# A fused attention and two-MLP kernel: the scores of four units read keys in place, the last two w_mid tiles are converted last, and the hand-written order of block 0 is replaced

## The chip, the cores and the metric

The kernel runs on one core of a Trainium2 chip. The metric is device time in microseconds (us), median of several executions. A core has a matrix engine (PE, with its weight loads shown as PEld), a vector engine (DVE), a scalar engine (ACT), a general engine (POOL) and SP, which here only issues DMAs. Each engine works through its own list of instructions in order and waits where an operand is not there yet.

## The reference, cut to what matters

```python
def reference(**kwargs):
    attn_out = _attn_ref(...)     # q, k, v: 4 x 8 heads x 768 x 64; 8 memory keys and values per head
    x = attn_out.transpose(0, 2, 1, 3).reshape(B * S, H * D)          # 3072 x 512
    x = maximum(maximum(x @ w1, x @ w2), x @ w3) @ w_mid              # 512 -> 768 -> 512
    h = x @ w_in                                                      # 512 -> 2048
    g = where(h >= 1, h, where(h <= -1, 0, (h + 1) ** 2 / 4))
    return g @ w_out                                                  # 2048 -> 512

def _attn_ref(q, k, v, mem_k, mem_v):
    for c in range(nc):           # 24 chunks of 32 queries; keys from 16 before to 8 after the chunk, and 8 memory keys
        scores = scale * q_c @ concat(mem_k, k_ctx).T
        a = exp(scores - max(scores)); a = a / (sum(a) + 1e-9)
        out[:, :, c_start:c_end] = a @ concat(mem_v, v_ctx)
```

## The kernel before, in words

The 3072 tokens are six blocks of 512; a block is four attention units of 128 tokens, so there are 24 units. Every matmul of the MLPs is done as three passes on operands split into a rounded high part and a low rest (`mm3`, lines 499 to 501), so every weight tile must first be converted on the chip.

**Weights of the first MLP.** w1, w2, w3 and w_mid (in the profile their fetches are `in_moe_w_dram` and `in_moe_w_out_dram`) are cut into 24 tiles of 512 KB, fetched by `f0` to `f23`; two neighbouring tiles make a pair q, and pair 0 to pair 11 go through the steps `wa` (ACT, L134), `wr` (ACT, L138), `wc` (three DVE instructions, L142, L143, L145), `wd` (DVE, L150), `wh` (ACT, L199) and `ws` (DVE, L204). Only two pairs can be staged at once: the fetch of pair q+2 waits for `wd` of pair q. The list `round1` sets which tile is which: before, a0, a1, a2, b for each of six columns f, where a0, a1, a2 are w1, w2, w3 and b is w_mid.

**An attention unit u** goes through loads `lk`, `lq` (keys, queries, 256 KB each) and `lv` (values, eight DMAs of up to 56 KB); key transposes `tk` (PE, L273), copy `ck` (ACT, L276), the edges shared with the neighbouring unit `ek`; query transposes `tq` (L304) and copy `cq` (L366); `kw` (ACT, L298, and once per batch L287), which lays the memory keys and the four overlapping windows of keys side by side; scores `s` (64 small instructions, L378); `mx` (DVE, L392, L393); `ex` (ACT, L397); `n` (DVE, L401 to L404); transposes `a` (L410) and copy `ca` (L414); `o` (64 small instructions, L426); `cx` (ACT, L436) and `dx` (DVE, L440), which write the high and low part of the MLP's input.

**Block 0.** `PLAN` is one list of step names, written out by hand; a program emits the steps in that order, and each engine gets its own part of it in that order. It holds units 0 to 7, the first step of unit 8, the conversion of all 12 pairs, the first layer of block 0 (`l0` to `l17`, 12 matmuls each, three `l` per column f; `lt` is the running maximum, `lh` the split) and its second layer (`m0` to `m5`, 12 matmuls each; column f needs w_mid's tile f). `d3` and `d7` are four matmuls without a use. `l0` needs pair 0 and all four units of block 0 (`dx3`), so it is the first matmul of the MLPs.

**After the plan** `order` lists slots of 12 matmuls for blocks 1 to 5: `slot_l1(j, f, m)` and `slot_l2(j, f)`. Each slot also takes one step of the attention of later units (`att_step`; two in slots 2 and 3), up to two `evictions` of a finished second layer, and one part of the conversion of a pair of the second MLP (`round_step`, `BY_PART`).

Of the kernel before, what the change touches and what calls it, by code (L numbers as in the profile page):

```python
# [37 lines left out]


PLAN = """  # L40
d3 lk1 d3 lmem0 d3 d3 lk0 d3 lm0 lq0 lv1 tk1 mem0 ck1 tk0 ck0 ek1 tq0 lk2 kw0 d3 mv2 cq0 lq1 lk3 s0
mv0 mx0 lq2 tk2 mv1 ck2 ek2 lk4 tq1 ex0 lv0 cq1 n0 tk3 kw1 ck3 s1 ek3 a0 kw2 mx1 tq2 lq3 tk4 cq2 f0
ck4 f1 s2 ex1 lk5 f2 d3 ek4 mx2 f3 kw3 lq4 lv2 ca0 n1 tq3 ex2 o0 cq3 n2 a1 cx0 s3 ca1 dx0 wa0 mx3 o1
wr0 tk5 wc0 a2 cx1 d7 d7 ca2 d7 ex3 d7 dx1 ck5 d7 d7 ek5 wd0 kw4 n3 wa1 tq4 f4 cq4 lv3 wc1 wr1 s4
wh0 o2 kw5 wd1 a3 d7 cx2 d7 ws0 f5 wh1 d7 lq5 f6 dx2 ca3 f7 mx4 lk7 o3 lv4 ws1 ex4 d7 cx3 d7 n4 wa2
tq5 wr2 dx3 a4 wc2 cq5 ca4 s5 l0 wa3 wd2 wr3 mx5 f9 l1 f8 wh2 lv5 wc3 ex5 lt0 o4 n5 l2 cx4 lt1 ws2
lq7 a5 lq6 wd3 ca5 l3 lm1 wa4 dx4 lk6 f11 lt2 wr4 f10 wc4 l4 lh2 lt3 wh3 wd4 tq7 o5 cq7 ws3 f13 wh4
f12 tk6 mv6 l5 cx5 ws4 lk8 ck6 lv6 dx5 wa5 lt4 tq6 lt5 wr5 m0 wc5 cq6 lh5 wa6 l6 wd5 wr6 wc6 lq8 f14
wh5 f15 tk7 l7 lt6 lk9 ck7 ws5 ek7 kw6 wd6 l8 lt7 f16 wh6 f17 ws6 s6 lt8 wa7 m1 mx6 wr7 wc7 lh8 ex6
tq8 l9 cq8 wa8 wd7 m2 wr8 wc8 f18 f19 lt9 wh7 l10 wd8 ws7 f21 wh8 f20 n6 tk8 l11 ck8 ek8 lt10 kw7  # L50
ws8 wa9 tk9 lt11 l12 wr9 wc9 ck9 wa10 a6 lh11 wd9 l13 ek9 wr10 f22 f23 wc10 ca6 lt12 m3 wh9 wd10 o6
ws9 wh10 s7 lt13 cx6 lv7 ws10 wa11 l14 mx7 wr11 kw8 dx6 l15 lq10 lt14 ex7 lk10 wc11 lk11 lh14 lm2
lq9 l16 lt15 wd11 m4 n7 wh11 ws11 a7 lt16 l17 ca7 o7 lt17 lh17 s8 cx7 dx7 m5 mx8 ex8 f24 f25 f26 f27
""".split()

ON_DVE = """
# [8 lines left out]
def attention_then_two_mlps(ctx, tc, q, k, v, mem_k, mem_v, w1, w2, w3, w_mid, w_in, w_out, out):  # L65
    nc = tc.nc
# [35 lines left out]
    weights = {}  # L102
    wsrc = {"a0": w1, "a1": w2, "a2": w3, "b": w_mid, "c": w_in, "d": w_out}
    wsrc = {n: w.bitcast(U32) for n, w in wsrc.items()}
    round1 = [(m, f) for f in range(K1) for m in ("a0", "a1", "a2", "b")]
    round2 = [(m, f + h) for m in "dc" for f in range(HF) for h in (0, HF)]
    conv = round1 + round2
    Q1, Q2, Q3 = len(round1) // 2, (len(round1) + K2) // 2, len(conv) // 2
# [106 lines left out]
    few = at.tile([P, 2 * HP, 1], F32, name="few")  # L215
    held = {"kw": None}
    qn, kn, pt, rs, aT, pm, pp, px = {}, {}, {}, {}, {}, {}, {}, {}
    xh, xl = {}, {}
# [151 lines left out]
    def st_s(u):  # L370

        ub = u % UPB
        t = [banks[i] for i in spots["s"]]
        for h in range(HP):
            for c in range(NC):
                for e in range(2):
                    r, i = slice(e * 64, e * 64 + 64), h % 2 * 2 + h // 2
                    nc.tensor.matmul(  # L378
                        t[e][c * CH:(c + 1) * CH, i * NK:(i + 1) * NK], qTb[u % 2][r, h, c], kw[r, h, c, 0:NK],
                        start=True, stop=True)  # L380
        b = spots["s"][0]
        pp["s", u] = sg = psums[:, b:b + 2, 0:HP * NK].rearrange("p e (h j) -> p e h j", h=HP)
        if ub == 0:
            nc.vector.memset(sg[0:CH, :, :, NM:NM + LEFT], FLOOR)
        if ub == UPB - 1:
            nc.vector.memset(sg[P - CH:P, :, :, NK - RIGHT:NK], FLOOR)

    def st_m(u):
        sg = pp.pop(("s", u))
        pt[u] = at.tile([P, 2 * HP, NK], F32, tag="p", name=f"p{u}", bufs=2)  # L390
        m, p = [x.rearrange("p (e h) j -> p e h j", e=2) for x in (few, pt[u])]
        nc.vector.tensor_reduce(out=m, in_=sg, axis=AX.X, op=ALU.max)  # L392
        nc.vector.tensor_tensor(out=p, in0=sg, in1=m.to_broadcast([P, 2, HP, NK]), op=ALU.subtract)  # L393

    def st_e(u):
        p = pt[u]
        nc.scalar.activation(out=p, in_=p, func=AF.Exp, scale=scale)  # L397

    def st_n(u):
        p = pt[u]  # L400
        nc.vector.tensor_reduce(out=few, in_=p, axis=AX.X, op=ALU.add)  # L401
        nc.vector.tensor_scalar(out=few, in0=few, scalar1=1e-9, scalar2=None, op0=ALU.add)
        nc.vector.reciprocal(out=few, in_=few)
        nc.vector.tensor_tensor(out=p, in0=p, in1=few.to_broadcast([P, 2 * HP, NK]), op=ALU.mult)  # L404
# [33 lines left out]
    def cp_xl(u):  # L438
# [54 lines left out]
    def att_step():  # L493
        for s in todo.pop() if todo else ():
            run(*s)
# [480 lines left out]
    with tc.manual_schedule(engines={ENG.PE, ENG.DVE, ENG.Activation, ENG.Pool, ENG.SP}):  # L976
# [67 lines left out]
        def w_tile(name):  # L1044
            return wpool.tile([P, 2, TB], F32, tag="w", name=name)

        last_block = done = 0
        for s, (f, *a) in enumerate(order):
            j = a[0]
            if f is not slot_l2 and j == NB - 1 and last_block == 0:  # L1050
# [28 lines left out]
            if last_block:  # L1079
                t = s - last_block  # L1080
                round_step(["out"])
                if t == 1:
                    for g in (2, 3):
                        hq["h22", g] = w_tile(f"h22_{g}")
                for name in LAST_BLOCK.get(t, "").split():
                    if name == "c":
                        split_c()
                    elif name == "raw":
                        load_c(loaded[0])
                        loaded[0] += 1  # L1090
                    elif name == "r":
                        load_d(t - 4)
                    elif name == "d":
                        i = len(resident)
                        split_d(i)
                        if i + 2 < len(RESIDENT):
                            load_d(i + 2)
                    elif name == "E":
                        hq["h21", 0] = w_tile("h21_0")
                    else:  # L1100
                        prep(0, name)
            else:
# [87 lines left out]
```

## Time and profile before

| | us |
|---|---|
| median of 3 runs (lowest, highest) | 962.3 (962.0, 962.8) |
| the profiled execution's own time | 960.31 |
| its span, first to last instruction | 958.5 |
| PE busy in the span | 938.7 |

The profiled execution has 1.8 us around its span. Times in the rows are counted from the span's start. A row of the timeline gives start, duration, engine, line, operation, what is written and read, the shapes and the number of merged instructions; in brackets the idle time of that engine before it and what ended it. An instruction may begin before the one ahead of it has fully ended, so the step from start to start is what a series costs.

### The profile page before, as it was taken

To read this page: it belongs to the slowest core of one execution; us is meant where nothing else is said; L and a number is where in the kernel's file an instruction comes from. 1 tells how busy PE (TensorE), PEld (TensorE's weight loads), DVE (VectorE), ACT (ScalarE), POOL (GpSimd) and SP (SyncE) were. 2 spreads that over 40 slices of the span, in tenths; PEclk is the share of its full clock that TensorE was granted. 3 is DMA by queue.
4 is the path that set the end of the run, shared out by engine and by line. 5 is a ranking of instruction groups with operands and counts; after the bars stand their busy time and mean duration, and the time that the engine had idled before them with its cause. 6 is when DMAs were issued, how large, how long until landed. Compare 5 with 4: busy or idle time off the path is not lost.

```text
span 958.5 us, 18892 instructions
## 1 busy us (share of the span) xinstructions
PE 938.7 (98%) x7090; PEld 772.4 (81%) x7090; DVE 704.6 (74%) x1001; ACT 541.9 (57%) x972; POOL 339.6 (35%) x330
## 2 busy tenths in 40 slices
PE   6799999999999999999999999999999999999998
PEld 5588887888888888888888888888888888888886
DVE  3999857687877777753337778997777988777855
ACT  5767554333343324223447777776777776777763
POOL 0000003221321111111746555555565555655642
PEclk8999999999999999999999999999999999999999
DMA  7896635676657677343414229524326744232823
GB/s 180 233 228 204 181 111 158 167 214 198 198 157 202 170 190 238 107 136 110 134 58 136 80 81 306 168 34 110 93 84 199 221 119 95 88 94 85 261 66 67
DMA packets 245900, 142.81 MB, mean 149 GB/s; under 512 B 174513, under 2 KB 223537, under 8 KB 245809
## 3 DMA queue, kind: packets, MB, share of 16 engines
q1 hardware_dynamic: 245808, 141.60, 51.9%
q8 instruction: 56, 0.92, 0.4%
q14 instruction: 36, 0.29, 0.1%
HBM read 109.71 MB, written 31.46 MB: 147 GB/s over the span
## 4 chain that ended last, share of the span: by engine, by line
PE 93%; DVE 4%; SPq 1%; DMA 1%; ACT 1%; issue 0%; POOL 0%; DVEq 0%; POOLq 0%
PE psums L499 29%; PE psums L501 29%; PE psums L500 29%; PE psums L426 2%; PE psums L378 2%; PE psums L410 1%; DMA kq<-in_k_dram 1%; PE psums L273 1%; DVE c L150 0%; PE psums L1011 0%; DVE p L404 0%; DVE p L393 0%; DVE few L392 0%; PE psums L304 0%; SPq L360 0%
## 5 line engine op out<-in xcount | busy, mean ns | idle before, releaser
L518 POOL TENSOR_TENSOR hl_a<-t,hh_a 128x512 fp32r<-128x512 f32 x30 | 41.5, 1383 | 384.6 <-ACT hh_a L516 384.6
L499 PE MATMUL psums<-xh,hi 128*128 128x512 f32 x432 | 172.2, 399 | 0.0
L501 PE MATMUL psums<-xh,lo 128*128 128x512 f32 x432 | 168.7, 390 | 0.0
L500 PE MATMUL psums<-xl,hi 128*128 128x512 f32 x432 | 168.2, 389 | 0.2 <-DVE xl L440 0.2
L810 POOL TENSOR_TENSOR hb<-h,hb 128x512 fp32r<-128x512 f32 x72 | 99.8, 1386 | 92.2 <-PE psums L501 59.5
L802 ACT CAST hb<-h 128x512 fp32r<-128x512 f32 x144 | 88.8, 622 | 48.1 <-PE psums L500 45.9
L534 DVE TENSOR_TENSOR t<-psums,t 128x512 f32<-128x512 f32 x72 | 49.4, 686 | 66.7 <-PE psums L501 66.7
L629 POOL TENSOR_TENSOR hb<-ra,hb 128x256 fp32r<-128x256 f32 x96 | 75.2, 796 | 58.8 <-ACT hb L628 53.8
L501 PEld LDWEIGHTS psums<-xh,lo 128*128 128x128 f32 x432 | 81.1, 188 | 17.8 <-DVE lo L204 0.3
L499 PEld LDWEIGHTS psums<-xh,hi 128*128 128x128 f32 x432 | 81.1, 188 | 16.5
L500 PEld LDWEIGHTS psums<-xl,hi 128*128 128x128 f32 x432 | 81.2, 188 | 16.4 <-DVE xl L440 0.6
L694 ACT ACTIVATE psums<-h 128x512 f32<-128x512 f32 x96 | 57.9, 603 | 60.0 <-DVE h L780 23.6
L501 PE MATMUL psums<-t,hb 128*128 128x512 f32 x192 | 74.8, 390 | 0.0
L499 PE MATMUL psums<-t,hb 128*128 128x512 f32 x192 | 74.7, 389 | 0.0
L500 PE MATMUL psums<-t,hb 128*128 128x512 f32 x192 | 74.7, 389 | 0.0
L629 POOL TENSOR_TENSOR hb<-rb,hb 128x256 fp32r<-128x256 f32 x72 | 55.5, 778 | 39.5 <-ACT hb L628 39.5
L808 DVE TENSOR_TENSOR hb<-psums,hb 128x512 fp32r<-128x512 f32 x66 | 44.9, 680 | 24.8 <-PE psums L501 20.3
L695 ACT ACTIVATE psums<-psums 128x512 f32<-128x512 f32 x96 | 55.9, 582 | 3.1
L499 PE MATMUL psums<-hh_a,hi 128*128 128x512 f32 x144 | 57.5, 399 | 0.0
L835 DVE TENSOR_TENSOR h<-h,h 128x1024 f32<-128x1024 f32 (+1 forms) x42 | 56.5, 1367 | 0.0
L501 PE MATMUL psums<-hh_a,lo 128*128 128x512 f32 x144 | 56.2, 390 | 0.0
L500 PE MATMUL psums<-hl_a,hi 128*128 128x512 f32 x144 | 56.2, 390 | 0.0
(145 smaller groups left out, 2235.9 us busy)
## 6 DMA issues: line engine op xcount, KB each, us to landing
ra<-cd SPq DMA_DIRECT2D x24, 512.0 KB
st<-in_moe_w_out_dram SPq DMA_DIRECT2D x22, 512.0 KB
t<-sd SPq DMA_DIRECT2D x21, 512.0 KB
st<-in_moe_w_dram SPq DMA_DIRECT2D x18, 512.0 KB
vw<-in_v_dram SPq DMA_DIRECT2D x152, 56.0 KB
st<-in_moe_w_in_dram SPq DMA_DIRECT2D x16, 512.0 KB
sd<-st SPq DMA_DIRECT2D x8, 896.0 KB
h<-yd SPq DMA_DIRECT2D x12, 512.0 KB
```

The costliest lines, as they stand in the source:

```text
L499: nc.tensor.matmul(out, whi, xhi, start=first, stop=False)
L500: nc.tensor.matmul(out, whi, xlo, start=False, stop=False)
L501: nc.tensor.matmul(out, wlo, xhi, start=False, stop=last)
L518: e.tensor_tensor(out=lo, in0=h, in1=hi.bitcast(F32), op=ALU.subtract)
L534: nc.vector.tensor_tensor(out=cur["t", j, f], in0=s, in1=cur["t", j, f], op=ALU.max)
L629: nc.gpsimd.tensor_tensor(out=c[:, 1], in0=t, in1=c[:, 0].bitcast(F32), op=ALU.subtract)
L694: nc.scalar.activation(out=a, in_=x, func=AF.Relu, bias=0.5, scale=0.5)
L695: nc.scalar.activation(out=a, in_=a, func=AF.Square)
L802: nc.scalar.copy(out=hi, in_=x)
L808: nc.vector.tensor_tensor(out=lo, in0=y, in1=hi.bitcast(F32), op=ALU.subtract)
L810: nc.gpsimd.tensor_tensor(out=lo, in0=x, in1=hi.bitcast(F32), op=ALU.subtract)
L835: nc.vector.tensor_tensor(out=x, in0=y, in1=z, op=op)
```

## The change: what it does

1. **Scores.** For units 0 to 3 (`DIRECT = 4`) the steps `kw0` to `kw3` are gone; each of a unit's 32 score matmuls (head pair, chunk, half) becomes two, one against the 8 memory keys (`memkT`) and one against a window of 56 keys in `kTb`; the profile shows two instructions for each of these f32 matmuls, so 128 in place of 64.
2. **Weight order.** In `round1` the w_mid tiles of f = 4 and 5 are last: pair 8 is a0, a1 of f=4, pair 9 is a2 of f=4 with a0 of f=5, pair 10 is a1, a2 of f=5, pair 11 the two w_mid tiles. `m4` and `m5` leave the plan: slot list `order` has, for block 1 and f=0, l1, l1, second layer (0, 4), l1, second layer (0, 5).
3. **Loop bookkeeping.** Two slots more, so one `att_step` in each; the parts of `round_step` follow `(s + 1) % 6`; two fetches fewer lie in the plan (26 for 28).
4. **The plan.** A new order; `lv` is cut into `vs`, two DMAs per chunk; 15 `d3` in place of 7 `d3` and 11 `d7`.
5. `ROWS = 0` leaves its new branches unused; a tile `sums` of 32 bytes per partition and one ACT copy of one column at the start are added.

```diff
-    round1 = [(m, f) for f in range(K1) for m in ("a0", "a1", "a2", "b")]
+    round1 = [(m, f) for f in range(K1) for m in ("a0", "a1", "a2", "b") if m != "b" or f < K1 - 2]
+    round1 += [("b", f) for f in range(K1 - 2, K1)]
...
+    def load_vs(x):
+        load_v(x // NC, (x % NC,))
...
-    def load_v(u):
+    def load_v(u, chunks=range(NC)):
         b, s0 = divmod(u, UPB)
-        for c in range(NC):
+        for c in chunks:
...
-                    nc.tensor.matmul(
-                        t[e][c * CH:(c + 1) * CH, i * NK:(i + 1) * NK], qTb[u % 2][r, h, c], kw[r, h, c, 0:NK],
-                        start=True, stop=True)
+                    keys = [kw[r, h, c, 0:NK]]
+                    if u < DIRECT:
+                        keys = [memkT[r, h, u // UPB], kTb[u % 2][r, h, c * CH:c * CH + WIN]]
+                    for n, x in enumerate(keys):
+                        j = i * NK + n * NM
+                        nc.tensor.matmul(
+                            t[e][c * CH:(c + 1) * CH, j:j + x.shape[-1]], qTb[u % 2][r, h, c], x, start=True, stop=True)
...
-    fetched, rounded, kept = [2 * Q1 + 4], [Q1], []
+    fetched, rounded, kept = [2 * Q1 + 2], [Q1], []
...
+        nc.scalar.copy(out=few[:, 0], in_=ident[:, 0:1])
...
+                if j == 1 and f == 0:
+                    order += [(slot_l2, 0, K1 - 2), (slot_l1, j, f, 2), (slot_l2, 0, K1 - 1)]
+                    continue
...
-                for _ in range(2 if s in (2, 3) else 1):
-                    att_step()
-                    done += 1
+                att_step()
...
-                part = 5 if s == 3 else done % 6
+                part = (s + 1) % 6
                 feed((5, 6, 4, 6, 5, 1)[part])
-                round_step(BY_PART[part].split() + (["a"] if s == 1 else []))
+                round_step(BY_PART[part].split())
```

The new plan up to the first steps of the MLP, and its end:

```
d3 d3 d3 d3 d3 f0 lk0 lmem0 f1 lm0 wa0 lq0 lk1 f3 d3 d3 d3 d3 mem0 wc0 tk0 f2 ck0 mv0 lk2 d3 tq0 tk1
mv1 wr0 lq2 cq0 wd0 ck1 vs1 ek1 s0 wh0 mx0 ws0 wa1 lk3 ex0 lq1 d3 tk2 wc1 ck2 wr1 f4 wd1 tq2 cq2 d3
d3 tq1 n0 f5 vs0 vs6 vs4 vs2 cq1 ek2 vs3 tk3 s1 a0 mx1 lk4 wa2 mv2 lq3 ck3 ek3 ca0 wr2 d3 s2 vs8 ex1
wc2 o0 vs7 lk5 mx2 tk4 n1 cx0 vs5 lq4 wd2 vs10 wh1 d3 tq3 ck4 cq3 a1 ex2 ek4 ca1 dx0 s3 tk5 wh2 ck5
n2 mx3 o1 vs11 tq4 cx1 lk6 ek5 vs9 a2 ex3 vs13 lq5 ca2 dx1 vs15 n3 cq4 tk6 o2 kw4 vs14 a3 vs12 cx2
ws1 ca3 lk7 s4 lm1 dx2 f6 f7 tq5 kw5 f9 mx4 ws2 o3 ck6 cq5 cx3 dx3 vs18 s5 tk7 ex4 ck7 vs16 l0 lq6
mx5 wa3 l1 wr3 ek7 n4 wc3 f8 a4 lt0 ...
... l16 f25 vs31 wc11 o7 lt15
wd11 l17 lh14 f24 wh11 cx7 dx7 ws11 lt16 lt17 tq8 kw8 cq8 s8 lh17 mx8 lk10 ex8 lq10
```

On PE the old plan has, ahead of `l0`, units 0 to 5 up to their scores, `a0` to `a4`, `o0` to `o3` and all the `d`; the new one has the same with `tk6` and `tk7` more and `a4` less.

## Rows read from the trace of the kernel before

**Rows 1.** The page: busy time by engine, and the chain that ended last

```profile
PE 938.7 (98%) x7090; PEld 772.4 (81%) x7090; DVE 704.6 (74%) x1001; ACT 541.9 (57%) x972; POOL 339.6 (35%) x330
...
PE 93%; DVE 4%; SPq 1%; DMA 1%; ACT 1%; issue 0%; POOL 0%; DVEq 0%; POOLq 0%
```

**Rows 2.** Windows: stretch, length, busy us by engine, PE clock, DMA share, GB/s

```profile
0.00:24.00 24.00, 16.44 (x274) 12.57 (x277) 8.04 (x22) 12.56 (x26) 0.85 (x8) 0.86 0.78 181
24.00:46.90 22.90, 15.83 (x519) 13.25 (x514) 22.00 (x36) 18.26 (x27) 0.00 (x0) 1.00 0.86 231
46.90:125.30 78.40, 78.40 (x786) 63.92 (x778) 71.36 (x93) 49.22 (x68) 0.00 (x0) 1.00 0.73 199
```

**Rows 3.** Timeline of PE around the first L1 matmul

```profile
44.81 0.66 PE L304 MATMUL psums<-ident,kq 128*128 128x128 f32 x4 [1.52 <-DMA kq<-in_q_dram]
...
46.93 0.50 PE L499 MATMUL psums<-xh,hi 128*128 128x512 f32 x1
```

**Rows 4.** Timeline of DVE, 40 to 50 us

```profile
40.99 0.68 DVE L392 TENSOR_REDUCE few<-psums 128x8 f32<-128x512 f32 x1
...
42.31 1.22 DVE L204 TENSOR_TENSOR lo<-c,hi 128x1024 fp32r<-128x1024 f32 x1
43.44 0.68 DVE L401 TENSOR_REDUCE few<-p 128x8 f32<-128x512 f32 x1
...
45.21 0.68 DVE L440 TENSOR_TENSOR xl<-psums,xh 128x512 fp32r<-128x512 f32 x1
45.81 0.68 DVE L142 TENSOR_SCALAR c<-c 128x1024 f32<-128x1024 f32 x1
...
47.26 1.23 DVE L145 SCALAR_TENSOR_TENSOR c<-st,c 128x1024 uint32<-128x1024 uint32 x1
...
48.62 1.22 DVE L150 CUSTOM_DVE_ANT_0 c<-st,c 128x2048 uint16<-128x2048 uint16 x1
```

**Rows 5.** Windows of 4 and 8 us before the first L1 matmul

```profile
0.00:8.00 8.00, 6.20 (x32) 4.78 (x33) 1.54 (x10) 1.87 (x2) 0.85 (x8) 1.00 0.69 155
...
12.00:16.00 4.00, 1.13 (x5) 0.71 (x4) 2.75 (x6) 2.65 (x6) 0.00 (x0) 0.67 1.02 214
16.00:20.00 4.00, 3.52 (x75) 3.06 (x76) 1.25 (x2) 2.16 (x5) 0.00 (x0) 0.50 0.74 163
...
24.00:32.00 8.00, 5.69 (x212) 4.84 (x207) 7.59 (x15) 6.23 (x11) 0.00 (x0) 1.00 1.12 282
```

**Rows 6.** Timeline of all engines: issue of f0 and f1, and wa0

```profile
19.90 1.12 SPq L121 DMA_DIRECT2D st<-in_moe_w_dram  x2
...
27.08 1.13 ACT L134 ACTIVATE c<-st 128x1024 f32<-128x1024 f32 x1 [0.27 <-DMA st<-in_moe_w_dram]
```

**Rows 7.** Timeline: the 64 instructions of s2 and of o2

```profile
21.14 0.86 PE L378 MATMUL psums<-kw,qTb 64*32 64x64 f32 x64 [0.24 <-ACT qTb L366]
...
36.26 1.14 PE L426 MATMUL psums<-aT,vxl 64*64 64x32 f32 x64
```

**Rows 8.** Groups by line, ACT, 0 to 47 us: busy, mean ns

```profile
L298 ACT COPY kw<-kT 128x896 f32<-128x896 f32 x6 | 5.6, 937 | 0.1
```

**Rows 9.** Timeline of PE: a key transpose, then two L1 steps to s6

```profile
73.45 0.60 PE L273 MATMUL psums<-ident,kq 128*128 128x128 f32 x4
73.80 0.47 PE L499 MATMUL psums<-xh,hi 128*128 128x512 f32 x1
...
79.44 0.86 PE L378 MATMUL psums<-kw,qTb 64*32 64x64 f32 x64
```

**Rows 10.** Timelines of DVE and PE: ws3 and ws4, and the matmul using ws3

```profile
63.83 2.42 DVE L204 TENSOR_TENSOR lo<-c,hi 128x1024 fp32r<-128x1024 f32 x2
...
65.10 0.50 PE L501 MATMUL psums<-xh,lo 128*128 128x512 f32 x1
```

**Rows 11.** Timelines of DVE and PE in block 1: wd of pair 12, and a9

```profile
142.04 1.21 DVE L150 CUSTOM_DVE_ANT_0 c<-st,c 128x2048 uint16<-128x2048 uint16 x1
...
149.59 0.63 PE L410 MATMUL psums<-ident,p 128*128 128x128 f32 x4 [0.80 <-DVE p L404]
```

More of the change, by code (lines that the diff above doesn't have):

```diff
@@ L31 @@
 TRIO0 = 12
+ROWS = 0
+DIRECT = 4
 LEAST, MOST = 2.0 ** -15, float.fromhex("0x1.dffffcp+16")
 PLAN = """
[L41 to L53, printed above, removed]
+d3 d3 d3 d3 d3 f0 lk0 lmem0 f1 lm0 wa0 lq0 lk1 f3 d3 d3 d3 d3 mem0 wc0 tk0 f2 ck0 mv0 lk2 d3 tq0 tk1
@@ new lines @@
+mx5 wa3 l1 wr3 ek7 n4 wc3 f8 a4 lt0 ex5 vs19 lt1 wa4 vs21 kw6 vs22 l2 wd3 wh3 n5 ca4 wr4 lt2 l3 wc4
+wd4 vs17 a5 lk8 f10 o4 lt3 ws3 cx4 vs20 tq6 wh4 ws4 l4 ca5 f11 tk8 lh2 vs23 dx4 f13 f12 lt4 cq6 s6
+wr5 ck8 mx6 wa5 ex6 wa6 wc5 lk9 o5 ek8 l5 cx5 mv6 lq7 wd5 kw7 vs24 lt5 l6 f15 dx5 f14 wh5 vs25 wr6
+wc6 lt6 wd6 vs26 wh6 vs27 tq7 ws5 lq8 l7 lt7 lh5 tk9 ws6 m0 f17 l8 wa7 l9 wr7 wc7 wd7 lt8 ck9 f16
+wa8 m1 wr8 n6 wc8 lt9 wh7 a6 f18 lk11 ca6 ek9 f19 ws7 cq7 wd8 lh8 l10 wr9 wh8 lt10 s7 lq9 f21 l11
+ws8 mx7 lt11 o6 wa9 ex7 vs28 vs30 wc9 m2 wd9 l12 cx6 wh9 f20 f23 n7 dx6 ws9 lm2 lt12 f22 lh11 wa10
@@ L54 @@
+wr10 wc10 l13 wd10 l14 a7 m3 wh10 vs29 wa11 lt13 wr11 l15 ca7 lt14 ws10 l16 f25 vs31 wc11 o7 lt15
+wd11 l17 lh14 f24 wh11 cx7 dx7 ws11 lt16 lt17 tq8 kw8 cq8 s8 lh17 mx8 lk10 ex8 lq10
 """.split()
@@ L215, in attention_then_two_mlps @@
     few = at.tile([P, 2 * HP, 1], F32, name="few")
+    sums = at.tile([P, 2 * HP, 1], F32, name="sums")
     held = {"kw": None}
@@ L392, in st_m @@
         nc.vector.tensor_reduce(out=m, in_=sg, axis=AX.X, op=ALU.max)
-        nc.vector.tensor_tensor(out=p, in0=sg, in1=m.to_broadcast([P, 2, HP, NK]), op=ALU.subtract)
+        if u < ROWS:
+            nc.vector.tensor_scalar(out=few, in0=few, scalar1=-scale, scalar2=None, op0=ALU.mult)
+            pp["e", u] = sg
+        else:
+            nc.vector.tensor_tensor(out=p, in0=sg, in1=m.to_broadcast([P, 2, HP, NK]), op=ALU.subtract)
     def st_e(u):
         p = pt[u]
-        nc.scalar.activation(out=p, in_=p, func=AF.Exp, scale=scale)
-    def st_n(u):
[L400 to L404, printed above, removed]
+        if u < ROWS:
+            sg = pp.pop(("e", u))
+            for h in range(2 * HP):
+                nc.scalar.activation(out=p[:, h], in_=sg[:, h // HP, h % HP], func=AF.Exp,
+                                     bias=few[:, h], scale=scale, accum_out=sums[:, h])
+        else:
+            nc.scalar.activation(out=p, in_=p, func=AF.Exp, scale=scale)
+    def st_n(u):
+        p, n = pt[u], sums if u < ROWS else few
+        if u >= ROWS:
+            nc.vector.tensor_reduce(out=n, in_=p, axis=AX.X, op=ALU.add)
+        nc.vector.tensor_scalar(out=n, in0=n, scalar1=1e-9, scalar2=None, op0=ALU.add)
+        nc.vector.reciprocal(out=n, in_=n)
+        nc.vector.tensor_tensor(out=p, in0=p, in1=n.to_broadcast([P, 2 * HP, NK]), op=ALU.mult)
     def st_a(u):
@@ L442, in attention_then_two_mlps @@
     parts = {
-        "lk": load_k, "lq": load_q, "lv": load_v, "lm": load_mv, "mv": fill_mv,
+        "vs": load_vs, "lk": load_k, "lq": load_q, "lv": load_v, "lm": load_mv, "mv": fill_mv,
         "tk": st_k, "ck": cp_k, "ek": edge_k, "kw": fill_kw,
@@ L486, in run @@
                 parts[kind](i)
-        elif kind in WEIGHTS or i < NU:
+        elif kind in WEIGHTS or i < (NU * NC if kind == "vs" else NU):
             parts[kind](i)
@@ L1045, in w_tile @@
             return wpool.tile([P, 2, TB], F32, tag="w", name=name)
-        last_block = done = 0
+        last_block = 0
         for s, (f, *a) in enumerate(order):
```

## The prediction, made before the changed kernel was run

> **What bounds the kernel now.** I read the page first. PE is busy 938.7 of 958.5 us, and 93% of the chain that ended last runs over PE [rows 1], so after it has started nothing else sets the time. The windows say when that is: before 46.9 us PE has work for only 16.44 and 15.83 us, much of it the idle matmuls `d`; from 46.90 to 125.30 it is busy for all 78.40 us [rows 2]. The timeline puts the first L1 matmul at 46.93; `tq5` just ahead of it waited for a DMA [rows 3]. The time is therefore the start of `l0`, plus PE's work behind it, plus what gaps open there. What holds the start? DVE is busy 22.00 of the 22.90 us before `l0`, but only 8.04 in the first 24 us [rows 2]. It is the full engine of the second half of the lead-in, while in the first half it has almost nothing: f0 and f1 are issued at 19.90, and the first conversion step, `wa0`, can begin at 27.08 only [rows 6]. Lead-in work that DVE could do early comes late.
>
> **The price of DVE's steps,** from start to start in one unbroken stretch [rows 4]: `mx` 40.99 to 42.31, 1.32 us; `ws` 42.31 to 43.44, 1.13; `n` 43.44 to 45.21, 1.77; `dx` 45.21 to 45.81, 0.60; `wc` from 45.81 to the end of L145 at 48.49, 2.68; `wd` 1.22. A pair costs 5.03, a unit 3.69.
>
> **The new plan on DVE.** Up to `dx3` it holds three whole pairs (before: two and part of a third), five `mx`, four `n`, four `dx`: 15.1 + 6.6 + 7.1 + 2.4 = 31.2 us. Three moments decide when that ends.
>
> First, pair 0. Ahead of f1's end lie f0, lk0, the memory keys and f1: 1.38 MB. DMA moved 155 GB/s in the first 8 us, 214 when it carried mostly small pieces, 282 where weight tiles were among them [rows 5]; 155 x 8 us at 214 GB/s means that it flowed from about 2.2 us. So f1 lands between 7.1 and 8.6; I take 8.0. `wa0` lasts 1.13 [rows 6], and `wc0` starts at 9.1.
>
> Second, pair 2. Nine steps follow on DVE (wc0, wd0, mx0, ws0, wc1, wd1, n0, mx1: 13.3 us), with some 0.7 us of waits for `s0` and its PSUM fill; DVE is free for `wc2` at 23.1. It needs f4 and f5, behind 5.3 MB in all (six tiles, lk0 to lk3, lq0 to lq2, the memory rows and their four small fills, vs1). From 2.2 us on that is 21.1 at 282 GB/s and 27.0 at 214; by the old execution's own pace (181 GB/s for 24 us, then 282) 27.4 [rows 2, 5]. Six tenths of it are weight tiles, so I lean to the fast end; not all the way, because SP stops at `mv0` until the memory values have landed behind f1, with lk2, mv1, lq2, vs1, lk3, lq1 and then f4 queued behind it. (f4's own wait, for `wd0`, is over by 13.) I take 24.0. `wa2` ends at 25.1, so DVE stands still for 2.0 us. ACT has `ck3`, `ek3`, `ca0` behind `wa2`, and so `s2` and `o0` on PE wait too; they are not needed on DVE before `mx2`, 2.7 us later.
>
> Third, the rest: 17.8 us of DVE to the end of `dx3`, plus 0.7 for small waits (4% as in the old stretch [rows 2]). That gives 43.6. I followed the other engines along it: the last values, vs12, are 8.4 MB in, 38.6 us at the old 231 GB/s [rows 2]; `o3`, `cx3` stand at 40 to 42; `tk7` needs lk7, 0.26 MB later. None ends after DVE. `l0` starts at 43.6 in place of 46.93: **-3.3 us**. With every DMA at its fast end and no wait it would be 40.1, with f5 at 27.4 it is 47.0.
>
> **Scores in place.** The four `kw` copies of 0.94 us leave ACT [rows 8], where nothing in the chain above waits for them. The old trace has no split score step. The lower bound for one is today's 0.86 us (same columns), the upper 1.73 (twice the instructions). `o` has as many instructions with half the columns and is not shorter, 1.14 us [rows 7]: instructions count, not columns, so I take 1.7. For four units that is 3.5 us more on PE, in a stretch where PE has 7 us without work; of `s0` 0.9 us lies ahead of `mx0`, and is in the 0.7 above. Keys are now held in `kTb` until `s`: `ck2` to `ck5` come after `s0` to `s3` in every list, so nothing new waits. The one-column copy at the start ends long before the first `ck`. [...]
>
> **PE behind l0.** The same steps, but `tk6` and `tk7` now lie ahead and `a4` behind: one transpose step less, from 73.45 to 73.80 [rows 9], **-0.35**. `m4` and `m5` are the same 24 matmuls in another place. Their four copies and stores move by four slots; the next second layer starts three slots after m5, 8 us, against four copies of 512 columns, each shorter than the 0.94 us of 896 [rows 8]. SP has as many DMAs for values as before, in smaller groups, so that a group's wait for a free buffer (`o` of an earlier unit) holds up less behind it.
>
> **The stall in block 1.** `a9` waited 0.80 us for DVE, which from 142.04 on had done `wd` of pair 12 and its combination between `mx9` and `n9` [rows 11]. In the new slot order that part falls in slot 4, one slot ahead of `s9`, which has moved to slot 5; `n9` gets free: **-0.8**. If I misread the slots, 0.
>
> **Supply behind l0.** DVE is busy 71.36 of 78.40 us there [rows 2], and before the weights came just in time: `ws3` and `ws4` ran from 63.83, and the first matmul on the low part started at 65.10 [rows 10]. In the new order the tightest is pair 9 for `l14`. Ahead of it PE has 17 steps of 2.82 us (two from 73.80 to 79.44 [rows 9]), seven transposes, three `o`, two `s`: 55.5 us. DVE has seven pairs, three `mx`, four `n`, three `dx` and 11 steps of `lt` and `lh` of the size of `dx`: 54.6. A margin of 0.9, where DVE's small waits (4% again) come to 2.2: I take a stall of **+0.5**, since a late pair holds PE once and the next is due later; bounds 0 and 3, twice the 1.3 by which those waits pass the margin. Pair 11 is not due until `m4`, so the old end of this race (`l17`) is relaxed.
>
> **Sum.** -3.3 - 0.35 - 0.8 + 0.5 = -3.95. The profiled execution, 960.3, would become 956.4; it lies 2.0 under the median, so the median goes from 962.3 to 958.3. Ends of the terms: -6.8 - 0.35 - 0.8 = -8.0 and 0.1 - 0.35 + 3 = +2.7.
>
> **Rivals.**
> *The tiles come in time.* f5 lands before 22, DVE never stands still, `l0` at 40.1 to 41.6: 954.8 to 956.3. For it: DMA at 282 GB/s. Against: small fills kept DMA at 155 at first.
> *Starved behind l0.* DVE loses its 4% and the margin of 0.9 is spent three or four times (pairs 5, 7, 9, 10): +3 in place of +0.5, 960.8. For it: rows 10. Against: pair 2 is done before `l0` now, and DVE begins that stretch 1.1 us richer.
> [...]
> *Weights ahead of keys (slower).* Pair 2's `wa2` stands in ACT's list ahead of `ck3`, `ek3`, and `wc2` in DVE's ahead of `mx2`: if f4 and f5 are late, all attention stops. f0 and f1 took 7 us from issue to use behind a full queue [rows 6]. Each us after 24.0 is a us of `l0`; the gain is gone when f5 lands at 28.0, at 31 it is 965.3. Against: 4.3 MB had moved by 24 us even at a DMA share of 0.78 [rows 2].
> *No change in effect* needs f5 near 27.4, the old pace: 962.
>
> **How the numbers follow.** Forecast as summed, `l0` at 41.6 to 45.7: 0.50, range 956.3 to 960.4. Tiles in time 0.17; starved 0.12; clock 0.06; old pace 0.05; late 0.10. A measurement here tells 0.2%, 1.9 us. Faster: 0.50 + 0.17 + half of starved = 0.73; the same: half of starved, clock and old pace, 0.17; slower (f5 past 29.8): 0.10. For eight in ten I cut the outer half of the late case and the best of the fast one: 954.3 to 962.8.
>
> **What would show it.** `wa0` near 8 and `wa2` near 24 us; DVE busy well over 15 us in the first 24; the first L1 matmul at 41.6 to 45.7; `s0` to `s3` at 1.6 to 1.8 us; no idle time before `a9`; under 1 us of PE idle from `l0` to the end of block 0, at full clock. I am wrong if `wa2` lies past 27, if DVE waits elsewhere ahead of `dx3`, or if PE shows waits for `hi` and `lo`.

## The result, and the profile after

The changed kernel takes 971.7 us (median of 4 executions, 970.5 to 974.2), the kernel before on the same chip 962.2: a ratio of 1.0104, with a 95% interval of 1.0081 to 1.0127. It is slower by 1%. I had forecast 958.3, and a range that ended at 962.8. The profiled execution took 971.35 us, 11.04 more than the one shown of before.

The page, as in [rows 1], with the line on the DMA queue of kind `instruction` beside it:

```profile
PE 946.8 (98%) x7334; PEld 779.4 (80%) x7334; DVE 705.6 (73%) x1001; ACT 537.6 (55%) x969; POOL 338.8 (35%) x330
...
q8 instruction: 58, 0.95, 0.4%
...
PE 91%; DVE 4%; issue 2%; DMA 1%; ACT 1%; SPq 1%; POOL 0%; DVEq 0%; ACTq 0%; POOLq 0%
```

"issue" in the chain, time in which an engine waited for nothing that the profile shows, has gone from 0% to 2%. The windows up to the first L1 matmul and behind it, as in [rows 2]:

```profile
0.00:24.00 24.00, 18.46 (x345) 13.96 (x346) 14.12 (x27) 10.95 (x18) 0.85 (x8) 0.93 1.00 240
24.00:54.30 30.30, 20.48 (x689) 17.33 (x686) 19.38 (x32) 17.02 (x32) 0.00 (x0) 0.79 0.80 195
54.30:125.30 71.00, 69.00 (x626) 56.44 (x624) 64.40 (x85) 44.63 (x62) 0.00 (x0) 0.97 0.61 169
```

DVE did its early work early: 14.12 us in the first 24, before 8.04, where the forecast asked for well over 15. But then it is busy for only 19.38 of 30.30 us, and PE too stands still for 9.8. The timeline of DVE, as in [rows 4], shows where:

```profile
9.62 0.69 DVE L146 TENSOR_SCALAR c<-c 128x1024 f32<-128x1024 f32 x1
...
25.30 0.69 DVE L146 TENSOR_SCALAR c<-c 128x1024 f32<-128x1024 f32 x1 [0.54 <-ACT c L138]
...
34.56 0.69 DVE L463 TENSOR_TENSOR xl<-psums,xh 128x512 fp32r<-128x512 f32 x1 [2.15 <-PE psums L1035]
...
41.80 0.69 DVE L463 TENSOR_TENSOR xl<-psums,xh 128x512 fp32r<-128x512 f32 x1 [2.24 <-ACT xh L459]
...
49.26 0.69 DVE L463 TENSOR_TENSOR xl<-psums,xh 128x512 fp32r<-128x512 f32 x1
53.65 0.11 DVE L398 MEMSET psums<- 32x64 f32 x1 [3.70 <-PE psums L391]
```

Up to `wc2` the plan runs as worked out: `wc0` at 9.62 (forecast 9.1), `wc2` at 25.30 (forecast 25.1). Then `dx0` and the memset of `s5` (L398) wait for PE, `dx1` waits for ACT's `cx1`, which stands behind `o1` on PE, and `dx3` starts at 49.26 where I had it end at 43.6. The chain that ended with the first L1 matmuls says what PE did (start, us, what):

```profile
21.70 1.63 PE psums L391 x49
...
27.50 0.23 PE psums L449 x2
27.73 2.89 issue
30.62 1.93 PE psums L449 x34
...
38.21 0.83 PE psums L449 x46
39.04 1.58 issue
40.62 0.53 PE psums L449 x18
...
48.79 0.43 PE psums L391 x24
49.22 3.43 issue
52.65 0.91 PE psums L391 x40
53.56 1.04 PE psums L281 x4
```

In the middle of `o0`, of `o1` and of `s5`, series of 64 small instructions each, PE stops for 2.89, 1.58 and 3.43 us, 7.90 in all, with nothing to wait for (the chain has one more of 0.58 us at 25.12, in `s2`). The windows from the span's start into each of the three stops count what PE had done by then (columns as above):

```profile
0.00:29.00 29.00, 21.13 (x476) 15.94 (x477) 18.44 (x33) 14.98 (x25) 0.85 (x8) 0.92 0.92 219
0.00:40.00 40.00, 29.09 (x732) 22.84 (x732) 25.47 (x45) 20.39 (x35) 0.85 (x8) 0.87 0.87 204
0.00:51.00 51.00, 37.30 (x986) 29.81 (x986) 32.88 (x56) 27.97 (x50) 0.85 (x8) 0.87 0.88 213
```

From stop to stop there are 256 and then 254 more matmuls, and 255 and 254 more weight loads (some records are missing). And 7,334 matmuls with 7,334 loads in 58 packets of the instruction queue, 0.95 MB, are 253 instructions and 16 KB a packet (the kernel before, with 7,090, has 56 packets). So two such packets lie between one stop and the next; I take them for blocks of PE's code. The DMA view around each stop (27.5 to 30.7, 38.0 to 40.7, 49.2 to 52.7 us) has one packet of that queue; its columns are packets, MB, share:

```profile
q8 instruction: 1, 0.02, 1.9%
...
q8 instruction: 1, 0.02, 2.2%
...
q8 instruction: 1, 0.02, 2.0%
```

The first and the third packet begin inside their stop, at 28.00 and 50.00 us; the second begins at 38.36, 0.7 us ahead of its stop, and ends in it at 39.31. My reading is that PE ran out of code; the part on why the prediction was wrong has the evidence from all the traces. The clock was also at half when `l0` began: the granted clock fell from 1.00 to 0.50 at 51.6 us, in the third stop, and rose again at 58.5. In the timeline of PE, as in [rows 3], the first nine L1 matmuls take 3.98 us; nine at 0.23 take 2.07. The half clock there (the granted clock of 54.3 to 125.3 is 0.97) costs 1.9 us. That the stops bring the clock down is not shown: at the first stop it fell as the stop began, both at 27.73 us, and e3 below had a granted clock of 0.61 over 26.5 us with no stop.

```profile
54.26 0.77 PE L522 MATMUL psums<-xh,hi 128*128 128x512 f32 x1
...
57.81 0.63 PE L524 MATMUL psums<-xh,lo 128*128 128x512 f32 x1
58.24 0.50 PE L522 MATMUL psums<-xh,hi 128*128 128x512 f32 x1
58.58 0.40 PE L523 MATMUL psums<-xl,hi 128*128 128x512 f32 x1
58.81 0.39 PE L524 MATMUL psums<-xh,lo 128*128 128x512 f32 x1
```

Behind `l0` there is one more long wait. Timelines of DVE and of PE around `o6`, and `a9` of [rows 11]:

```profile
101.52 1.23 DVE L208 TENSOR_TENSOR lo<-c,hi 128x1024 fp32r<-128x1024 f32 x1 [0.64 <-ACT hi L203]
102.66 0.68 DVE L404 TENSOR_REDUCE few<-psums 128x8 f32<-128x512 f32 x1
103.37 0.69 DVE L409 TENSOR_TENSOR p<-psums,few 128x512 f32<-128x512 f32 x1
...
104.12 1.23 PE L449 MATMUL psums<-aT,vw 64*64 64x32 f32 x64 [2.00 <-DVE p L409]
...
160.13 0.60 PE L433 MATMUL psums<-ident,p 128*128 128x128 f32 x4
```

From `m0` on, `s` and `o` share PSUM banks 4 and 5, so `o6` may not write before `mx7` has read the scores of `s7`; `mx7` stands behind `ws8`, which waited for ACT. `a9` waits no more. The account of the profiled executions: `l0` at 54.26 for 46.93, +7.3; its half clock +1.9; `o6` +2.0; a wait of `s8` +0.7; one transpose step less, -0.35; `a9` -0.8. Together +10.75, of the 11.04 measured. Both are single executions, and the start of `l0` scatters by some 3 us from one execution to the next, as the traces below show.

### The profile page after: what moved, and what is told of

It reads as the page before. It is cut to its first block, busy times and chain, and to the rows that moved or that the text cites. A ratio compares the mean times of both kernels' runs of the same rounds, so it can differ in the third digit from the quotient of the medians.

```text
span 969.6 us, 19359 instructions
## 1 busy us (share of the span) xinstructions
PE 946.8 (98%) x7334; PEld 779.4 (80%) x7334; DVE 705.6 (73%) x1001; ACT 537.6 (55%) x969; POOL 338.8 (35%) x330
## 4 chain that ended last, share of the span: by engine, by line
PE 91%; DVE 4%; issue 2%; DMA 1%; ACT 1%; SPq 1%; POOL 0%; DVEq 0%; ACTq 0%; POOLq 0%
PE psums L522 28%; PE psums L524 28%; PE psums L523 28%; PE psums L449 2%; PE psums L391 2%; PE psums L433 1%; PE psums L1035 1%; DVE c L154 1%; DMA st<-in_moe_w_dram 1%; DVE lo L208 1%; DVE c L149 1%; PE psums L281 0%; DVE t L557 0%; PE psums L312 0%; DVE c L146 0%
```

## The experiments

Times are medians; each ratio is to the kernel before on the same chip. My theory after the result was that the split scores use up PE's code faster than it comes. Rivals were PE's own time in these steps, and the new order by itself.

**e1: the change, keys copied.** `DIRECT = 0`, and in the plan

```diff
-ek1 s0 ... ek2 vs3 tk3 s1 ... ek3 ca0 wr2 d3 s2 ... ek4 ca1 dx0 s3
+ek1 kw0 s0 ... ek2 kw1 vs3 tk3 s1 ... ek3 kw2 ca0 wr2 d3 s2 ... ek4 kw3 ca1 dx0 s3
```

> The changed kernel with the keys of units 0 to 3 copied side by side again (kw0 to kw3 stand behind ek1 to ek4), so that each score step has 64 PE instructions in place of 128; all else stays. Theory 1 (PE runs dry of instructions: it stopped for 2.9, 1.6 and 3.4 us at its 961st, 1473rd and 1985th instruction, with nothing to wait for, while a block of 16 KB of code was on its way): 512 fewer loads and matmuls (two blocks) before l0, the stops shrink to 2 us or less in all, the first L1 matmul starts at 46 to 49 us in place of 54, and the time falls to 963 to 967. Theory 2 (the new order of loads and of DVE's work delays the attention; the number of PE's instructions does not matter): the four copies of 0.94 us come on top, 971 to 974. Theory 3 (the half clock alone): as theory 2, since idle matmuls and order are unchanged.

Measured: 966.1, ratio 1.0046 (1.0031 to 1.0061), 5.6 us less than the change. `l0` came at 45.67; no stop is left ahead of it. The rest of the change still costs 4 us: `o6` waited 1.45 us, `s8` 0.68, two stretches of 3.4 us at half clock lie behind `l0`, and `a5` waited 2.37 us, because the copy `ca4`, which must come first, stands behind `wa4` on ACT, and that waited for a late tile:

```profile
59.82 0.66 PE L433 MATMUL psums<-ident,p 128*128 128x128 f32 x4 [2.37 <-ACT aT L437]
```

**e2: the old plan, scores in place.** The kernel before with the new inner loop of `st_s`, without `kw0` to `kw3`, and with `ck3 ek3` and `ck4` behind `s1` and `s2`.

> The kernel before with the score edit alone: units 0 to 3 read keys in place, kw0 to kw3 leave the plan, ck3, ek3 and ck4 stand behind the scores that read the buffer they write. Theory 1: two blocks of code more before l0 at some 4 us a block, partly hidden: the first L1 matmul at 50 to 54 us, 965 to 970. Theory 2: no loss, 961 to 963, since only the copies leave. Theory 3: the d7 are still there, no loss.

**e4: the old plan, unused matmuls.** The kernel before; beside each score matmul of units 0 to 3 one of 8 columns into unused PSUM:

```diff
+                    if u < 4:
+                        nc.tensor.matmul(
+                            t[e][c * CH:(c + 1) * CH, TB // 2 + i * NM:TB // 2 + (i + 1) * NM], qTb[u % 2][r, h, c],
+                            kw[r, h, c, 0:NM], start=True, stop=True)
```

> The kernel before with 32 more matmuls of 8 columns in each score step of units 0 to 3, written to unused columns and read by nobody; keys are still copied. It adds to PE what the score edit adds, 512 instructions with their loads, and nothing else. Theory 1: 965 to 970, as with the score edit in the old plan. Theory 2 (instructions matter only by PE's own time, 0.9 us in each of four steps in a lead-in where PE has 7 us without work): 962 to 964.

Measured: 967.4 (ratio 1.0059, 1.0039 to 1.0079) and 967.5 (1.0061, 1.0039 to 1.0083). The doubled instructions cost 5.7 us in the old plan too, whether they read keys in place or do nothing. In both, PE stopped, in e2 for 0.6 us and in e4 for 3.0 us; the window up to that stop of e4 holds

```profile
0.00:30.00 30.00, 21.30 (x603) 17.31 (x604) 11.71 (x30) 15.71 (x30) 0.85 (x8) 0.89 0.78 190
```

603 is 127 more than the 476 of the change's first stop: the next block end, in another step (`s3`). I took that for proof of the theory. It is not: e4 adds PE time as well as instructions.

**e3: the change, fewer instructions.** For units 0 to 3 one matmul against the memory keys serves all four chunks, 80 matmuls a step in place of 128:

```diff
+            for e in range(2 if u < DIRECT else 0):
+                r, j = slice(e * 64, e * 64 + 64), (h % 2 * 2 + h // 2) * NK
+                nc.tensor.matmul(
+                    t[e][:, j:j + NM], qTb[u % 2][r, h].rearrange("p c t -> p (c t)"), memkT[r, h, u // UPB],
+                    start=True, stop=True)
```

> The changed kernel with one matmul of all 128 queries against the 8 memory keys per head pair and half, in place of one per chunk: 80 PE instructions per score step in place of 128 (64 before), columns as before. Theory 1: between the changed kernel and the run with copied keys, first L1 matmul at 48 to 52, 964 to 969. Theory 2: no change, 971 to 972.

Measured: 966.1, ratio 1.0046 (1.0029 to 1.0063). No stop ahead of `l0`, which came at 50.48. The step was no shorter, though. In the timeline of `s1`, the memory matmuls with 128 query columns as weights take 0.08 us each, the others 0.016:

```profile
21.99 0.39 PE L385 MATMUL psums<-memkT,qTb 64*128 64x8 f32 x4 [0.24 <-ACT qTb L374]
22.31 0.33 PE L398 MATMUL psums<-kT,qTb 64*32 64x56 f32 x16
...
24.41 0.80 PE L440 MATMUL psums<-ident,p 128*128 128x128 f32 x3
```

2.4 us a step, more than the change's 1.63, and still 5.6 us faster than the change: fewer instructions helped, more PE time did not undo it. The clock did not help either. The window from 24 us to `l0` has PE busy for 26.45 of 26.50 us, at a granted clock of 0.61:

```profile
24.00:50.50 26.50, 26.45 (x617) 22.27 (x615) 19.48 (x31) 16.60 (x32) 0.00 (x0) 0.61 0.84 203
```

The keys are still read in place here. So of all the runs this one parts the number of instructions most cleanly from PE's time, from the clock and from the way the keys are read.

**e5: the change, one swap.** In the plan:

```diff
-ws8 mx7 lt11 o6
+mx7 ws8 lt11 o6
```

> Whole change, with one swap: mx7 ahead of ws8 on DVE. If o6 waits because o6 and s7 share PSUM and mx7 stands behind ws8 (which itself waited 0.64 us), mx7 can begin at 100.9 in place of 102.7, the 2.00 us wait of o6 shrinks to about 0.2 and the time falls by 1.8 us, to about 970. If the wait is set elsewhere (by s7 or by PE being late), nothing changes: 971.7.

Measured: 969.7, ratio 1.0079 (1.0058 to 1.0100). The median is 2.0 us lower, but the intervals of the change and of e5 overlap. The trace has no wait of `o6`. It is of the shortest execution (964.6; the other four took 969.6 to 971.3): `l0` came at 50.30, behind stops at the same counts as in the change, but shorter ones (0.74, 1.00 and 1.90 us), and one more of 1.18.

**e6: parts 2 and 3 alone.** The kernel before with the new `round1`, `order` and bookkeeping; `m4 m5 f26 f27` leave the old plan.

> The kernel before with parts 2 and 3 alone: w_mid's last two tiles last, m4 and m5 as slots of block 1, new loop bookkeeping; old plan otherwise, scores copied. If the forecast's reading of the slots is right, a9 no longer waits 0.80 us and the time falls by 0.8 us. If the tiles' order also relaxes the supply of weights at l14 to l17 nothing more shows, because PE had no waits there before. The rival is no change, a wait of the same size elsewhere in block 1.

Measured: 964.4, ratio 1.0020 (1.0009 to 1.0031): slower, against both expectations. The waits of PE from 100 to 400 us:

```profile
PE psums L411 <- DVE p L405: 1.4, 1, 1.4
PE psums L500 <- ACT xh L437: 0.7, 1, 0.7
```

`a9` no longer waits, but `a7` (1.4 us) and block 1's first matmul on unit 7's `xh` (0.7) do. `m4` and `m5` were 24 matmuls ahead of these; moved behind them, they no longer cover `n7` and `cx7`. Against the 0.8 us of `a9` that is 1.3 us more, of the 2.3 measured. In this trace `l0` came at 49.66, 2.7 us later than in the kernel before, though nothing ahead of it was changed.

**f1 and g: the change mended, with none and with two units in place.** f1 is e1 with four moves; in g units 0 and 1 read keys in place. In both, unit 8's query transposes overwrite unit 7's before these are copied, so unit 7 is computed with other queries; the work is the same.

```diff
-ex5 vs19 lt1 wa4 vs21 kw6 vs22 l2 wd3 wh3 n5 ca4 ... wa8 m1 wr8 ... ws8 mx7 ... ex7 vs28 ... lt17 tq8 kw8 cq8 s8
+ex5 ca4 vs19 lt1 wa4 vs21 kw6 vs22 l2 wd3 wh3 n5 ... wa8 tq8 m1 cq8 wr8 ... mx7 ws8 ... ex7 kw8 vs28 ... lt17 s8
```

> The change with copied keys (as in e1, 966.1) and four steps moved: mx7 ahead of ws8, ca4 ahead of wa4, tq8 and cq8 ahead of m1, kw8 behind ex7. If what e1 still loses lies in a5 (2.4 us), o6 (1.5), s8 (0.7) and in the two half-clock stretches of 3.4 us behind the first two stops (some 1.7 us each), it falls by 4.6 to 8 us: 958 to 961.5, with l0 unchanged near 45.7. If these waits only pass to other steps because DVE or the DMAs are late, it stays within 2 us of e1.

> As f1, but the scores of units 0 and 1 read keys in place: 128 more PE instructions ahead of l0 than f1, half of the change's. If PE's code supply sets the price, l0 comes 2 to 5 us later than in f1, with one or two stops in which PE waits for nothing, and the time rises by 2 to 5 us. If the price hung on something else of the last two units (their edges, their order), or the copy were the dearer way early on, g is no slower than f1.

Measured: f1 961.2, ratio 0.9996 (0.9980 to 1.0011); g 961.8, 0.9999 (0.9987 to 1.0011). The moves gave 4.9 us. g had two stops, f1 one, and `l0` at 49.20 for 47.66, but the 2 to 5 us expected are not there: PE waited 4.0 us for two `kw` copies, in f1 5.9 for four.

**e7: the old plan, PE time with few instructions.** In each score step of units 0 to 3, eight unused 256-column matmuls, one after every eight scores.

> The kernel before with eight unused 256-column matmuls in each score step of units 0 to 3: about the PE time that the 32 unused small matmuls of e4 took (0.9 us a step), but 8 instructions a step more in place of 64. If what costs in e2 and e4 is the supply of PE's instructions, the time is within 1.5 us of before: 962 to 963.5, without a stop in which PE waits for nothing. If it is PE's time in the score steps, it is as slow as e4, +5 us: 967.

Measured: 971.0, ratio 1.0106 (1.0089 to 1.0123). The dose was wrong: set one by one among the scores, each unused matmul and its eight scores take 0.46 us or more, and `s0` took 4.2 us in place of 0.86 (0.46 us for each of the first five of its eight parts, 0.70, 0.69 and 0.56 for the last three):

```profile
9.88 0.32 PE L378 MATMUL psums<-kw,qTb 64*32 64x64 f32 x8 [1.28 <-ACT qTb L366]
10.12 0.28 PE L383 MATMUL psums<-ident 128*128 128x256 bf16 x1
10.34 0.32 PE L378 MATMUL psums<-kw,qTb 64*32 64x64 f32 x8
```

It shows one thing: in the old plan, PE time in these steps alone, some 13 us of it, moves `l0` by 9.6.

**e8 and e9: the right dose, in the old plan and in the new.** Seven unused matmuls together, in the middle of each score step of units 0 to 3; e8 is the kernel before, e9 is f2.

```diff
+            if u < 4 and h == 1:
+                bf = ident.bitcast(mybir.dt.bfloat16)
+                for _ in range(7):
+                    nc.tensor.matmul(t[0][:, TB // 2:], bf[:, 0:P], bf, start=True, stop=True)
```

**f2 and f3: the ends.** f2 is f1 with `cq7` behind `l7`, so that every unit has its own queries. f3 is f2 with the four units in place (`DIRECT = 4`, no `kw0` to `kw3`).

> As e7, but the unused 256-column matmuls stand together, seven between the two halves of a score step, where a row of them takes 0.125 us each: some 0.9 us and 7 instructions a step, as much PE time as e4 added with 64 instructions. e7 showed that PE time alone delays l0 (some 13 us more PE time, 9.7 us later). Instruction supply alone: within 1.5 us of before, 962 to 963.5. PE time at e7's rate, 3.6 us times 0.73: 964.5 to 965. PE time as the whole cause of e4: 967.

> f2 with e8's seven unused matmuls in each score step of units 0 to 3: the PE time of the split scores without their instructions, in the new plan. If the new plan has room for PE time and not for instructions, it is within 1.5 us of f2; if PE time is the cause, it is as slow as f3, 5 us or more over f2.

> f1 with unit 7's queries copied before unit 8's are transposed. The same work at the same places for the engines, so f1's time again: 960 to 962, no worse than before. A wait at cq7's new place would make it slower.

> f2 with all four units' scores in place, as in the whole change: e5 less the 0.7 us of s8, 968.5 to 969.5, some 8 us over f2, where two units in place (g) cost 0.6. If g was the truer measure of what an in-place unit costs, it is within 2 us of f2.

Measured: e8 967.5, ratio 1.0061 (1.0038 to 1.0084), the same as e4. Its timeline of `s0` shows the dose, 0.87 us:

```profile
10.47 0.46 PE L378 MATMUL psums<-kw,qTb 64*32 64x64 f32 x32 [1.60 <-ACT qTb L366]
10.86 0.94 PE L384 MATMUL psums<-ident 128*128 128x256 bf16 x7
11.73 0.45 PE L378 MATMUL psums<-kw,qTb 64*32 64x64 f32 x32
```

So in the old plan PE time alone costs as much as e2 and e4 do; the number of instructions need have no share. That it has none is not shown: `l0` came at 50.84 in e8, at 52.50 and 52.31 in e2 and e4, and e8 has PE at half clock for 3.4 us right behind `l0` (L1 matmuls 0.43 us apart, then 0.23), which these two have not. In the new plan it is the other way: f2 961.9 (0.9997, 0.9982 to 1.0011), e9 962.4 (1.0004, 0.9990 to 1.0017), f3 969.0 (1.0052, 1.0026 to 1.0079; two of its six executions, the traced one among them, lay near 963). The same PE time, with 1.1 us of short stops in it, costs nothing that can be told; the split scores cost 5 to 7 us. But e9 adds more than PE time: its clock was higher. The windows from 24 us to `l0`, first of f2, then of e9, have 0.84 and 0.93, so part of the time that the unused matmuls took came back:

```profile
24.00:49.20 25.20, 17.99 (x567) 15.12 (x565) 19.59 (x32) 18.48 (x33) 0.00 (x0) 0.84 0.74 175
```

```profile
24.00:48.70 24.70, 19.38 (x617) 15.02 (x614) 19.81 (x32) 18.44 (x33) 0.00 (x0) 0.93 0.75 180
```

PE's waits up to 60 us, first of f2, then of f3:

```profile
PE psums L391 <- ACT kw L306: 6.9, 4, 2.1
```

```profile
PE psums L449 <- issue: 4.2, 2, 2.4
PE psums L391 <- issue: 1.3, 1, 1.3
```

In place, 6.9 us of waits for the copies go, and three stops come, after the same instructions as in the change. In these two traces `l0` came at 49.18 and 51.88; no trace shows the four longer executions of f3.

How far one trace can be trusted: up to `l0`, the kernels e1, f1 and f2 are the same program, and `l0` came at 45.67, 47.66 and 49.18; so are the change, e5 and f3, with 54.26, 50.30 and 51.88; so are the kernel before and e6, with 46.93 and 49.66. The first two groups do not overlap, but one trace against one other, 3 us apart, shows little.

**h1 and h2: an earlier `l0`.** f2 with `s5`, `tk7`, `mx4`, `ws2` behind `dx3` and `l0`, `s4` behind `o3`, `ek5` behind `ex3`; h1 also has seven `d3` more ahead of `s0`, `s1`, `s2` and one less ahead of `tq3`. In both, `kw5` has come ahead of `s4`, so unit 4 is scored against unit 5's keys.

> The change with copied keys; unit 7's queries copied before unit 8's are transposed; mx7, ca4, tq8, cq8 and kw8 moved as in f1; s5, tk7, mx4 and ws2 behind dx3 and l0, s4 behind o3, ek5 behind ex3; seven d3 more in the gaps ahead of s0, s1 and s2, one less ahead of tq3. If l0 in f1 (47.7) was held by the stop of 1.2 us in s5, by s4 ahead of o3 (0.9) and by the half clock from 12.9 to 19.7 and from 23.1 to 33.4, l0 comes at 43.5 to 45.5 and the time is 957 to 959, below both kernels. If the fillers' instructions cost more than the clock gives back, it is no faster than h2.

> As h1 without the fillers. If s5 and s4 are what held l0 in f1, l0 comes at 45 to 46.5 and the time is 958.5 to 960.5; if other steps are late by as much, it stays at f1's 961.

Measured: h1 965.4, ratio 1.0040 (1.0023 to 1.0056); h2 963.3, 1.0017 (1.0008 to 1.0026). In h2 `l0` came at 43.78, where my forecast had it, and the kernel is no faster than f2. `s5` and `tk7` now lie behind `l0`, and DVE and ACT are not ready there (PE waits 0.43 us for DVE, 0.99 and 0.35 for ACT): `l6` starts at 70.1, in f1, whose `l0` came 3.9 us later, at 70.6. In h1 the fillers moved a block's end to `l0` itself; timeline of PE:

```profile
49.23 0.50 PE L522 MATMUL psums<-xh,hi 128*128 128x512 f32 x1 [2.10 <-issue]
```

and the window up to 48 us:

```profile
0.00:48.00 48.00, 34.53 (x730) 27.27 (x730) 30.43 (x54) 31.07 (x53) 0.85 (x8) 0.89 0.88 200
```

730 is the place of the change's second stop, 732. Six fillers net, 24 matmuls, cost 2 us here; what they give to the clock (0.89 in this window, 0.81 in the first 45.5 us of f1) is worth less.

## Why the prediction was wrong

**The step that failed: scores in place, a term that the sum has at nothing.** I asked what 3.5 us of PE time would hide behind, and found 7 us without work. As far as the runs tell, that part held: `s1`, the one split step with no wait or stop of note inside, took 1.63 us where I had 1.7, and in e9 as much PE time cost nothing that can be told, though at a higher clock. What I left out is that a split step is 128 matmuls and 128 loads, as much as one 16 KB packet holds (253 by the page). The order of the steps was followed on every engine, the supply of their instructions on none. In the change's trace the stops are 7.9 of the 10.7 us by which `l0` missed 43.6; the rest is PE at half clock and small waits, not split further. By the medians, the 13.4 us between 958.3 and 971.7 are 5.6 for the split scores (the change against e1 and e3), 4.2 for what f2's moves repair (e1 to f2), and 3.6 that f2 itself lies above the forecast: with copied keys `l0` came at 45.7 to 49.2, not at 43.6.

The evidence for supply, not a hidden dependency: the stops fall in `o0`, `o1`, `s5`, `s3`, `l0`, by the count of instructions and not by the step; e3 parts instructions from time, and e9 against f3 agrees. The times of the single 16 KB packets, which the traces hold, bear it out. Number them from the span's start. The five stops of the change and of the kernel before, with the packet of each (us):

| kernel | matmuls before the stop | packet | begins | ends | PE goes on |
|---|---|---|---|---|---|
| change | 349 | 2 | 23.20 | 24.42 | 25.70 |
| change | 476 | 3 | 28.00 | 28.97 | 30.62 |
| change | 732 | 5 | 38.36 | 39.31 | 40.62 |
| change | 986 | 7 | 50.00 | 51.12 | 52.65 |
| before | 475 | 3 | 29.86 | 31.16 | 32.55 |

Over all 17 traces, a stop after some 348 matmuls goes with packet 2, after 476 with packet 3, after 603 with packet 4, and so on, one packet for each 128 matmuls and their loads. Up to 75 us there are 26 such stops, in 13 of the traces, of 0.3 to 3.4 us, and at every one PE goes on 1.2 to 1.7 us after the end of its own packet, 2.2 to 3.3 us after its start. And of the first nine packets of each trace none began before PE was in the block ahead of the one that it brings (0 to 137 matmuls ahead of that block's first by the records, some of which are missing; a block is 128). My reading of this is that PE had at most about one block in reserve: where 2.2 us or more pass from a packet's start to PE's going on, a block that is used up in 1.63 us is too short to cover the next one's coming.

[Rows 8] misled me too: the copies that I took as free were what PE waited for in f2, so the edit did have a gain of up to 6.9 us of waits, and gave it back.

**The lead-in on DVE** held while PE had code: `wc0` 9.6, `wa2` at 24.15 (forecast 24.0), `wc2` 25.3. Then my own sign of being wrong came true, DVE waiting elsewhere ahead of `dx3`. (The "nine steps" ahead of `wc2` are eight; their sum, 13.3, is right.) The rival "tiles in time" and the slower one "weights ahead of keys" did not occur; the slow end came by a mechanism that was no rival of mine.

**"The time is the start of l0, plus PE's work behind it"** is half true. h2 has `l0` at 43.8 and is not faster: DVE and ACT behind `l0` were not ready sooner. So even without the stops the -3.3 would have shrunk; f2, the new plan with copied keys and four repairs, equals the kernel before.

**Supply behind `l0`, +0.5:** no such wait for `hi` or `lo` is in the change's trace. What came was `o6`, +2.0, by the shared banks 4 and 5, which stand in the code and which I did not follow; in e5's trace, with `mx7` first, the wait is gone.

**The slow clock at `l0`** had 0.06 in the forecast. No run ahead of the forecast shows PE at half clock at `l0`; the chance was my estimate. What the change's run showed is a granted clock of 0.50 from 51.6 to 58.5 us, which cost 1.9 us behind `l0`. Why is open: it fell in the stop of `s5`, but f2, with no stop there, also began `l0` at half clock (47.9 to 51.3 us, its first L1 matmuls 0.42 to 0.58 us apart, then 0.23), and e1 did not (0.23 to 0.31 apart).

**`a9`, -0.8,** held in the change, and the slots were read rightly. e6 shows that the same edit on the old plan opens `a7` and block 1's first matmul, 1.4 and 0.7 us. I had called moving `m4` and `m5` free, and looked only at the evictions behind them, not at what they cover.

**One transpose less, -0.35,** stands in the account and was not tested by itself.

Open: what starts a fetch within the block ahead, and why PE goes on only 1.2 to 1.7 us after the packet's end; and why g, with two units in place, loses nothing although it stops.

## What to carry to other kernels

Where an edit multiplies small instructions, count them in blocks of code, not only in time: here 64 tiny matmuls and their loads were half of a packet's 253 instructions, and the change's packets 2 to 7 began 4.4 to 6.2 us apart (23.20 to 50.00 us), where a split score step used one up in 1.63 and at the stops 2.2 us or more passed from a packet's start to PE's going on. When a stop has no releaser, count the instructions up to it in several kernels: here a constant grid of 127 or 128 matmuls pointed to code, and the times of the packets agreed. And before crediting a start that comes sooner, look whether the engines that feed what follows are sooner too; work moved away from a place was also a cover for the waits there.

## What the runs showed of the hardware

PE stood still for 0.3 to 3.4 us, with nothing to wait for that the profile shows, at 26 places in the first 75 us of 17 traces (13 have one or more). The counts before these stops were 349, 476, 732 and 986 matmuls in the change, 603 in e2 and e4, 857 in g: 127 or 128, with as many weight loads, or a multiple of it apart. In the change and the kernel before, PE went on 1.28 to 1.65 us after the end of a 16 KB packet of queue 8, 2.26 to 2.69 after its start; that it had waited for code is my reading. None of the first nine packets of code of a trace began before PE was in the block ahead (0 to 137 matmuls ahead of the block that it brought). Even the kernel before has one such stop, 1.3 us in its fillers, with 475 matmuls done at 31.8 us. A score matmul with 8 columns took about as long as one with 56 or 64: 128 matmuls, half of them with 8 columns, took 1.63 us (0.0127 each), 64 with 64 columns 0.86 (0.0134). Eight scores and one bf16 matmul of 256 columns, taken in turn, took 0.46 us in each of the first five parts of e7's `s0`, where 0.86/8 and 0.87/7 make 0.23. The granted clock was 0.61 from 24.0 to 50.5 us of e3, with PE busy for 26.45 of these 26.50 us: if the clock was at 1.00 or 0.50, as in the change's trace, a busy PE had the half clock for some 78% of that stretch.
